# A gated feed-forward kernel: two sums moved up one place on VectorE, the last row tile copied out by two engines, and two late weight fetches split

## The chip, the cores and the metric

The kernel runs on one core of a Trainium2 chip. The metric is the device time of one execution, in microseconds (us). The 34 timed runs of the kernel before lie between 541.10 and 543.48 us, over all calls (a call is one session on one chip, in which kernels are timed in turn).

The engines are called PE (TensorE matmul), PEld (its weight loads, which overlap the matmuls), DVE (VectorE), ACT (ScalarE), POOL (GpSimd) and SP (SyncE, which issues all DMA transfers here). PSUM is the memory, in eight banks, into which PE writes its sums and out of which DVE and ACT read.

## The reference

```python
def reference(x, w_gate, w_up, w_down):          # x: 1 x 2048 x 1024, bf16; hidden size 3584
    g = jnp.einsum("bsd,df->bsf", x, w_gate)
    u = jnp.einsum("bsd,df->bsf", x, w_up)
    h = _gelu(g) * u                              # tanh form of gelu
    return jnp.einsum("bsf,fd->bsd", h, w_down)
```

## The kernel before

The kernel handles 1024 rows of `x` in each of two passes. It cuts every matrix product in 2 x 2 blocks and forms the four result blocks from seven block products in place of eight, with sums and differences of blocks made on DVE and POOL. A *unit* is such a 2 x 2 product for 256 hidden columns, for gate and up at once. A pass has 14 units and then the down-projection. In the code, `p1`, `u2` and `p5` are copies of PSUM banks that ACT makes (`snap`). "tb" and "sa" are operands of matmul products, and this document calls those groups of matmuls by them. A *keep cast* copies a block of `w_down` into a PSUM bank on ACT, and DVE then forms a difference from it (`keep_part`); there are three in a unit, in 12 units of the first pass. The parts that matter here (cuts are marked):

```python
    def unit(u, banks, xT, w, s, t, p1, after_p5, aside, keep, ahead_of_p4, snap_first):
        GU = range(2)                      # gate, up

        def add(ps, other):
            g = new(dve, ps[0], other[0], ADD, "sum", dtype=f32)
            dve(ps[1], ps[1], other[1], ADD)
            return g, ps[1]

        e, c, d = banks                    # three pairs of PSUM banks
        aside(-2)
        g, up = add(c, p1)                 # first block of this unit: the two sums
        ...
        for i in GU:
            product(e[i], s["s2"][i], t["t2"], False)
        ...
        keep(0, c[0])                      # first pass only
        ...                                # gelu(g), product g*up into hT
            u2 = [snap(e[i], "u2") for i in GU]
        keep(1, c[0])
        keep(2, c[1])
        c = d
        for i in GU:
            product(c[i], s["s1"][i], t["t1"], True)
        p5 = [snap(c[i], "p5") for i in GU]      # ACT copies the two banks out
        after_p5()
        for i in GU:
            product(e[i], s["s3"][i], t["t3"], False)
        ...
        for i in GU:
            product(c[i], s["s4"][i], t["tb"], False)   # adds onto the sums that p5 copied out
        times(2 * u + 1, 1, gelu(g), up)
        aside(1)
        g, up = add(c, u2)
        ahead_of_p4()                      # PE: first products of the next unit
        for i in GU:
            product(e[i], s["sa"][i], t["t4"], False)
        times(2 * u, 1, gelu(g), up)
        aside(2)
        times(2 * u + 1, 0, gelu(e[0]), e[1])    # the unit's last gelu and last product

    def keep_part(j, part, ps):            # differences of w_down blocks, made in the first pass only
        ...
        nc.scalar.copy(out=ps, in_=a)
        dve(made[j][:, part], ps, b, SUB)

    def fetch73(j):                        # one block of w_down, 256 KB, for each of j = 0 to 13
        raw[3, j] = slot([P, 2, N], bf16, "raw")
        nc.sync.dma_start(out=raw[3, j], in_=wdn[:, :, j, N:])

    # in down(), the last block of the output:
        def put21(i):
            store(ip, 1, i, 0, lambda st: nc.scalar.copy(out=st, in_=e[i]))

        if last:
            ...
            for i in I:
                for j in range(NJ):
                    matmul(e[i], sa[j][:, i * P : (i + 1) * P], q4[j], False, j == NJ - 1)
                put21(i)
```

DVE and PE run in the order in which the program is written. On ACT a scheduler sets the order, except in the very first unit.

## Time and profile before

| what | value | read from |
|---|---|---|
| time, median of 3 | 542.64 us (541.96 to 542.75) | the runs |
| span of the profiled run | 539.8 us | page |
| PE busy | 535.1 us, 99% | page |
| one unit, first pass | mostly 12.63 us | timeline, starts of the "sa" matmuls |
| one unit, second pass | 12.56 us | the same |
| last ACT copy, start and length | 536.37 us, 0.59 us | timeline |

The page's first part gives busy time, share of the span and number of instructions for each engine; its fourth part gives the chain of waits that ended last.

```profile
PE 535.1 (99%) x2414; PEld 379.5 (70%) x2414; DVE 334.9 (62%) x524; ACT 255.4 (47%) x463; POOL 239.2 (44%) x215
...
PE 99%; ACT 0%; DVE 0%; issue 0%
```

After the start PE is almost never visibly idle. That does not say that it is never late: the starts of its matmuls do. A unit is bounded by the first "sa" matmul of one unit and that of the next. The next view has the busy time of every engine in one unit of the first pass and in one of the second (columns: window, its length, then busy time and instructions of each engine, granted clock, DMA share, GB/s).

```profile
47.52:60.15 12.63, 12.63 (x59) 8.91 (x57) 8.36 (x14) 8.00 (x15) 12.63 (x12) 1.00 0.65 184
299.23:311.79 12.56, 12.56 (x58) 9.00 (x57) 6.56 (x11) 6.64 (x12) 9.05 (x9) 1.00 0.32 83
```

The same matmuls take 0.07 us longer in the first pass, where ACT and DVE have the keep casts and their differences to do as well. The timeline of that unit shows where (columns: start, length, engine, line, operation, output and input, count, and in brackets the idle time just before and what ended it).

```profile
48.83 0.60 ACT L179 ACTIVATE g<-bank 128x512 f32<-128x512 f32 x1 [1.48 <-PE bank L111]
...
49.82 0.69 DVE L90 TENSOR_TENSOR hT<-g,bank 128x512 bf16<-128x512 f32 x1 [1.75 <-PE bank L111]
...
50.42 0.68 DVE L90 TENSOR_TENSOR sum<-bank,p 128x512 f32<-128x512 f32 x1
...
51.14 0.59 ACT L274 CAST bank<-raw 128x512 f32<-128x512 bf16 x1 [1.71 <-DVE sum L90]
...
52.20 1.06 ACT L107 COPY u<-bank 128x512 f32<-128x512 f32 x2
...
53.14 1.12 ACT L274 CAST bank<-raw 128x512 f32<-128x512 bf16 x2
...
54.18 1.08 ACT L107 COPY p<-bank 128x512 f32<-128x512 f32 x2
54.89 1.70 PEld L111 LDWEIGHTS bank<-tb,s 128*128 128x128 f32 x8 [0.17 <-issue]
54.99 2.04 PE L111 MATMUL bank<-tb,s 128*128 128x512 f32 x8
```

Read it upwards. The weight load of the "tb" matmuls starts 0.17 us after the one before it ended, though the loads around it follow each other closely. The view names no releaser for this gap ("issue"), so what follows is read from the program. A load normally starts 0.22 us ahead of its matmul; here it is 0.10 (54.89 and 54.99), and about 0.07 us of the delay reaches the matmuls. The "tb" matmuls add into the banks that the p5 copies (54.18) read. Those stand on ACT behind two casts, two u2 copies, a gelu and the first cast (51.14), in one row without a gap. The first cast waited 1.71 us for DVE's sum, which ran at 50.42 because it stands behind the last product of the former unit (49.82), for which DVE had waited 1.75 us on PE.

The lines of the list of waits that belong to this (engine and line, what it waited for, us in total, times, longest):

```profile
DVE hT L90 <- PE bank L111: 43.7, 25, 1.8
...
ACT g L179 <- DVE sum L90: 28.6, 19, 1.7
...
ACT bank L274 <- DVE sum L90: 20.5, 12, 1.7
```

And the end of the kernel, from the timeline, and then SP's own wait for the last store (list of waits of SP's queue in the last 5 us):

```profile
536.37 0.59 ACT L413 CAST st<-bank 128x512 bf16<-128x512 f32 x1 [2.59 <-PE bank L111]
```

```profile
SPq L631 <- DMA out_dram<-st: 1.4, 1, 1.4
```

### The profile page before, as it was taken

To read this page: it belongs to the slowest core of one execution; us is meant where nothing else is said; L and a number is where in the kernel's file an instruction comes from. 1 tells how busy PE (TensorE), PEld (TensorE's weight loads), DVE (VectorE), ACT (ScalarE), POOL (GpSimd) and SP (SyncE) were. 2 spreads that over 40 slices of the span, in tenths; PEclk is the share of its full clock that TensorE was granted. 3 is DMA by queue.
4 is the path that set the end of the run, shared out by engine and by line. 5 is a ranking of instruction groups with operands and counts; after the bars stand their busy time and mean duration, and the time that the engine had idled before them with its cause. 6 is when DMAs were issued, how large, how long until landed. Compare 5 with 4: busy or idle time off the path is not lost.

```text
span 539.8 us, 7428 instructions
## 1 busy us (share of the span) xinstructions
PE 535.1 (99%) x2414; PEld 379.5 (70%) x2414; DVE 334.9 (62%) x524; ACT 255.4 (47%) x463; POOL 239.2 (44%) x215
## 2 busy tenths in 40 slices
PE   9999999999999999999999999999999999999997
PEld 5577777666677646888877667777777775488885
DVE  2986666666666895694945545445554459676730
ACT  3556666666656410255354555454555541114431
POOL 1079966677773500000097777777766600000000
PEclk9999999999999999999999999999999999999999
DMA  9766666666664899979772232233330059573751
GB/s 247 157 181 177 175 176 191 201 185 186 200 188 141 294 379 316 301 181 292 240 195 79 78 80 78 79 88 99 101 101 4 1 167 372 182 240 92 236 183 49
DMA packets 108133, 93.28 MB, mean 173 GB/s; under 512 B 17216, under 2 KB 92992, under 8 KB 108096
## 3 DMA queue, kind: packets, MB, share of 16 engines
q1 hardware_dynamic: 108096, 92.82, 58.8%
q8 instruction: 19, 0.31, 0.2%
q14 instruction: 18, 0.15, 0.1%
HBM read 74.45 MB, written 15.20 MB: 166 GB/s over the span
## 4 chain that ended last, share of the span: by engine, by line
PE 99%; ACT 0%; DVE 0%; issue 0%
PE bank L111 98%; PE bank L502 1%; PE bank L449 0%; ACT st L413 0%; DVE warm L433 0%
## 5 line engine op out<-in xcount | busy, mean ns | idle before, releaser
L93 POOL TENSOR_TENSOR s<-w 128x512 fp32r<-128x512 bf16 x102 | 120.0, 1198 | 165.1 <-DVE t L90 86.7
L111 PE MATMUL bank<-t,s 128*128 128x512 f32 x648 | 151.7, 390 | 0.0
L111 PEld LDWEIGHTS bank<-t,s 128*128 128x128 f32 x648 | 121.6, 188 | 25.5
L90 DVE TENSOR_TENSOR hT<-g,bank 128x512 bf16<-128x512 f32 x112 | 76.7, 687 | 92.9 <-ACT g L179 46.0
L111 PE MATMUL bank<-xT,w 128*128 128x512 bf16 (+1 forms) x504 | 111.9, 376 | 0.0
L107 ACT COPY p<-bank 128x512 f32<-128x512 f32 x124 | 70.6, 593 | 77.4 <-PE bank L111 77.1
L111 PEld LDWEIGHTS <-w 128*128 128x128 bf16 x504 | 47.0, 98 | 58.5 <-issue 6.9
L179 ACT ACTIVATE g<-sum 128x512 f32<-128x512 f32 x81 | 51.4, 635 | 29.8 <-DVE sum L90 28.6
L111 PE MATMUL bank<-q 128*128 128x512 f32 x240 | 58.9, 389 | 0.0
L111 PE MATMUL bank<-t,sa 128*128 128x512 f32 x216 | 58.8, 414 | 0.0
L93 POOL TENSOR_TENSOR s<-w,s 128x512 fp32r<-128x512 bf16 x50 | 57.8, 1181 | 0.0
L93 POOL TENSOR_TENSOR s<-s,w 128x512 fp32r<-128x512 f32 x50 | 57.0, 1162 | 0.0
L90 DVE TENSOR_TENSOR sum<-bank,p 128x512 f32<-128x512 f32 x54 | 37.0, 685 | 30.5 <-PE bank L111 30.5
L111 PE MATMUL bank<-tb,s 128*128 128x512 f32 x216 | 54.0, 392 | 0.0
L111 PEld LDWEIGHTS bank<-q 128*128 128x128 f32 x240 | 45.0, 188 | 9.4
L111 PE MATMUL bank<-raw,hT 128*128 128x512 bf16 x224 | 48.7, 379 | 0.0
L111 PEld LDWEIGHTS bank<-t,sa 128*128 128x128 f32 x216 | 40.7, 188 | 10.7
L111 PEld LDWEIGHTS bank<-tb,s 128*128 128x128 f32 x216 | 39.6, 188 | 9.9 <-issue 2.0
L102 ACT CAST tb<-raw 128x512 fp32r<-128x512 bf16 x28 | 17.2, 626 | 60.0 <-DMA raw<-in_w_down_dram 26.5
L90 DVE TENSOR_TENSOR q<-hT 128x512 fp32r<-128x512 bf16 x56 | 38.4, 686 | 4.5 <-PE bank L111 4.5
L111 PEld LDWEIGHTS <-hT 128*128 128x128 bf16 x224 | 21.8, 98 | 26.5 <-issue 0.5
L90 DVE TENSOR_TENSOR bank<-bank,p 128x512 f32<-128x512 f32 x54 | 37.4, 693 | 3.1 <-PE bank L111 3.1
(45 smaller groups left out, 454.7 us busy)
## 6 DMA issues: line engine op xcount, KB each, us to landing
raw<-in_w_down_dram SPq DMA_DIRECT2D x80, 256.0 KB, 4.8
q<-td SPq DMA_DIRECT2D x60, 256.0 KB, 5.0
w<-in_w_gate_dram SPq DMA_DIRECT2D x27, 512.0 KB, 5.9
w<-in_w_up_dram SPq DMA_DIRECT2D x27, 512.0 KB, 7.0
td<-m SPq DMA_DIRECT2D x12, 768.0 KB, 4.5
w<-td SPq DMA_DIRECT2D x6, 1024.0 KB, 9.7
out_dram<-st SPq DMA_DIRECT2D x32, 128.0 KB, 1.7
td<-w SPq DMA_DIRECT2D x2, 768.0 KB, 6.6
```

What stands on the lines that cost most here:

```text
L90: nc.vector.tensor_tensor(out=out, in0=a, in1=b, op=op)
L93: nc.gpsimd.tensor_tensor(out=out, in0=a, in1=b, op=op)
L102: nc.scalar.copy(out=t, in_=src)
L107: nc.scalar.copy(out=t, in_=ps)
L111: nc.tensor.matmul(ps, lhsT=lhs, rhs=rhs, start=start, stop=stop, skip_group_check=True)
L179: nc.scalar.activation(g, src, ACT.Gelu_apprx_tanh)
L502: nc.tensor.matmul(bank[3][:, :cols], lhsT=warm[:, :P], rhs=warm[:, :cols], start=True, stop=True)
```

## The change

Three small things, all meant to take waits off the path to PE or off the end. (1) The two sums that open a unit are recorded by the unit before it, ahead of its last product, so that DVE does them while it waits for PE. (2) The very last 128 x 512 copy out of PSUM is done half by ACT and half by DVE. (3) The last two of the fourteen `w_down` fetches of a stage are issued as two transfers each. The core of the diff:

```diff
-        g, up = add(c, p1)
+        g, up = c11()
 ...
         times(2 * u, 1, gelu(g), up)
-        aside(2)
+        behind_p4()
         times(2 * u + 1, 0, gelu(e[0]), e[1])
 ...
+            def behind_p4():
+                if "p1" in nxt:
+                    nxt["c11"] = add(cc, nxt["p1"])
+
+            def c11():
+                return nxt.pop("c11", None) or add(cc, p1)
 ...
     def fetch73(j):
         raw[3, j] = slot([P, 2, N], bf16, "raw")
-        nc.sync.dma_start(out=raw[3, j], in_=wdn[:, :, j, N:])
+        for kh in (range(2),) if j < NJ - 2 else (range(1), range(1, 2)):
+            kh = slice(kh.start, kh.stop)
+            nc.sync.dma_start(out=raw[3, j][:, kh], in_=wdn[:, kh, j, N:])
 ...
         def put21(i):
-            store(ip, 1, i, 0, lambda st: nc.scalar.copy(out=st, in_=e[i]))
+            def put(st):
+                h = N // 2 if last and i == NS - 1 else N
+                nc.scalar.copy(out=st[:, :h], in_=e[i][:, :h])
+                if h < N:
+                    nc.vector.tensor_copy(out=st[:, h:], in_=e[i][:, h:])
+
+            store(ip, 1, i, 0, put)
```

(`add` is moved out of `unit`, and `unit` takes `c11` and `behind_p4` as arguments; that is cut here.)

More of the change, by code (lines that the diff above doesn't have):

```diff
@@ L196, in raw_products, with add, unit @@
         return p1
-    def unit(u, banks, xT, w, s, t, p1, after_p5, aside, keep, ahead_of_p4, snap_first):
+    def add(ps, other):
+        g = new(dve, ps[0], other[0], ADD, "sum", dtype=f32)
+        dve(ps[1], ps[1], other[1], ADD)
+        return g, ps[1]
+    def unit(u, banks, xT, w, s, t, c11, after_p5, aside, keep, ahead_of_p4, behind_p4, snap_first):
         GU = range(2)
-        def add(ps, other):
-            g = new(dve, ps[0], other[0], ADD, "sum", dtype=f32)
-            dve(ps[1], ps[1], other[1], ADD)
-            return g, ps[1]
         e, c, d = banks
         aside(-2)
-        g, up = add(c, p1)
+        g, up = c11()
         aside(-1)
@@ L576 @@
             with tc.manual_schedule(engines={ENG.Activation}) if first else nullcontext():
-                unit(u, (e, cc, dd), xT, w, s, t, p1, prepare, aside, keep, ahead_of_p4, first)
+                unit(
+                    u, (e, cc, dd), xT, w, s, t, c11, prepare, aside, keep,
+                    ahead_of_p4, behind_p4, first,
+                )
             if u + 1 < NU:
```

## The prediction

> **What bounds the kernel.** TensorE: the page has PE busy 535.1 of 539.8 us, and the chain that ended last is 99% PE. The Trainium skill ("Perfetto Trace Analysis", Identifying the Most-Contended Engine) warns that pipelined matmuls make this busy time a poor measure, so I look at the starts of matmuls in the timeline. One f32 matmul of 512 columns starts every 0.227 us. Off that pace:
>
> - A unit takes 12.56 us in the second pass ("sa" matmuls at 299.23, 311.79 us) but mostly 12.63 in the first (47.52, 60.15, 72.78). The difference sits in the eight "tb" matmuls: 1.88 us in the first pass, 1.816 in the second; the "sa" group adds 0.01. In all about 0.75 us.
> - Only the first pass has the "keep" casts on ACT. From 51.14 us ACT has no gap: cast (after waiting 1.71 us for DVE's sum), gelu, two u2 copies, two casts, two p5 copies (54.18 to 55.26). The "tb" matmuls add into the banks that p5 empties; their weight load comes 0.17 us late ("issue") at 54.89. I infer that late p5 is the cause.
> - DVE's sum at 50.42 stands behind the last product of the former unit, for which DVE waited 1.75 us on PE, though the sum's own inputs were ready by about 47.
> - The end: the last ACT copy, 0.59 us at 536.37, then its store.
>
> **What the change does.** (1) The order of instructions has the two sums ahead of the last product on DVE in every unit; nothing is added. They should run at 48.0 to 49.3, in DVE's idle time; the last product can still run at 49.8. ACT's first cast moves to about 49.4 (behind the gelu at 48.83) and p5 to about 53.1, bounded then by PE's end of the u2 banks (about 51.5). That is 1 us of slack, so the "tb" stall vanishes: 0.7 us. In the second pass PE does not wait: nothing. (2) The last copy becomes 256 columns on ACT beside 256 on DVE. From 0.59 (ACT) and 0.69 us (DVE, two operands) for 512 columns and the clocks in "Trainium Kernel Development and Optimization", NeuronCore Architecture (1.2 and 0.96 GHz), halves are estimated at 0.38 and 0.42 us: 0.15 us off the tail. (3) The split fetches add four DMA issues, about 0.5 us each on SP; down-projection matmuls keep 0.907 us per four throughout, so no fetch is critical: zero.
>
> **On the critical path:** about 0.85 us, 0.16%. Predicted 541.8 us against 542.64; range 541.1 to 542.5. Faster by over 2%: 0.005; within 2%: 0.99; slower: 0.005.
>
> **What would show it.** First-pass units at 12.56 to 12.58 us, "tb" groups at 1.82; ACT's waits for DVE's sum (28.6 and 20.5 us in the list of waits) mostly gone; in that unit the first cast near 49.4 and p5 near 53.1; the last two copies near 0.4 us, ending within 0.1 us of each other; down-projection unchanged.
>
> **What would make it wrong.** The "tb" lag may not be p5's but come from shared memory ports or from DMA traffic; then only the tail gains. Two engines reading one PSUM bank at the end may slow each other, taking the 0.15 back. The spread of the runs (0.8 us) is as large as the effect: times alone may not show it, traces will.

## The result

The changed kernel took 541.64 us (median of 4, 541.34 to 541.75) against 542.67 for the kernel before in the same rounds (4 runs, 541.96 to 542.75). The ratio is 0.9983, with a 95% interval of 0.9966 to 1.0000. Ratios here and below are the mean time of one kernel's fast runs over that of the other's fast runs of the same rounds, so they are not quite the ratio of the medians. The mean difference is 0.92 us.

The profile after. First the page again:

```profile
PE 532.6 (99%) x2380; PEld 380.6 (71%) x2414; DVE 335.1 (62%) x525; ACT 259.9 (48%) x463; POOL 239.8 (44%) x215
...
PE 98%; DMA 1%; issue 0%; SPq 0%; DVE 0%; ACT 0%
```

PE seems to have 2.5 us less to do, but that is mostly a trap: 2380 matmuls are recorded in place of 2414, while the weight loads are still 2414. The edit takes no matmul away, so records are missing, not work. The second-pass units show it: they last 161.82 us in both traces, and PE's busy time in them falls from 161.82 to 161.00. About 0.78 of the 2.5 us is the wait that went away, which the profile had counted as busy, because it models the ends of matmuls (before, all 150.04 us of the first-pass units counted as busy). The durations of whole units do not suffer from missing records. The same two windows, one unit of each pass:

```profile
47.89:60.45 12.56, 12.49 (x58) 8.98 (x57) 8.39 (x14) 8.14 (x15) 12.56 (x12) 1.00 0.61 173
298.97:311.53 12.56, 12.49 (x57) 9.00 (x57) 6.47 (x11) 6.84 (x12) 9.03 (x9) 1.00 0.31 83
```

The first-pass unit now takes what the second-pass unit takes. The timeline of it (this kernel is 0.37 us later at this point, because its start was slower by about that much; subtract it to compare):

```profile
48.30 0.68 DVE L90 TENSOR_TENSOR sum<-bank,p 128x512 f32<-128x512 f32 x1
...
49.69 0.59 ACT L272 CAST bank<-raw 128x512 f32<-128x512 bf16 x1
...
50.18 0.69 DVE L90 TENSOR_TENSOR hT<-g,bank 128x512 bf16<-128x512 f32 x1 [0.59 <-PE bank L111]
...
53.45 1.08 ACT L107 COPY p<-bank 128x512 f32<-128x512 f32 x2
...
55.13 1.77 PEld L111 LDWEIGHTS bank<-tb,s 128*128 128x128 f32 x8
55.35 1.97 PE L111 MATMUL bank<-tb,s 128*128 128x512 f32 x8
```

The sum runs ahead of the product, DVE waits 0.59 us where it waited 1.75, the first cast no longer waits for a sum, p5 starts 1.1 us earlier in the unit (53.08 against 54.18 after subtraction), and the weight load of "tb" comes without a gap, 0.22 us ahead of its matmul. In the list of waits, in which the first cast's wait for the sum (20.5 us before) has gone:

```profile
DVE hT L90 <- PE bank L111: 13.6, 24, 0.6
...
ACT g L179 <- DVE sum L90: 7.6, 6, 1.7
```

The end, from the timeline, and then SP's own waits:

```profile
536.11 0.37 ACT L415 CAST st<-bank 128x256 bf16<-128x256 f32 x1 [2.59 <-PE bank L111]
536.51 0.42 DVE L417 CAST st<-bank 128x256 bf16<-128x256 f32 x1 [11.29 <-ACT st L415]
```

```profile
SPq L647 <- DMA out_dram<-st: 1.1, 1, 1.1
```

Two things are unlike the prediction. The halves of the last copy do not overlap: DVE was released by ACT (ACT's half raises semaphore 110, and DVE's half waits for it). And SP waits 1.1 us for the last store where it waited 1.4, although the store took as long to land as before.

Cut at the same events, the two spans compare like this. The stretches are: start to the first "sa" matmul; first-pass units, from there to the first down-projection matmul; first down-projection, from there to the first "sa" matmul of the second pass; second-pass units; second down-projection, to the start of the last copy; copy, from its start to the issue of the last store; end.

```
stretch (us)                 before   after   difference
start                         34.94   35.33    +0.39
first-pass units             150.04  149.26    -0.78
first down-projection        101.70  101.83    +0.13
second-pass units            161.82  161.82     0
second down-projection        87.87   87.88    +0.01
last copy to store's issue     0.61    0.86    +0.25
store's issue to end           2.80    2.53    -0.27
span                         539.78  539.50    -0.28
```

The start and the first down-projection vary from run to run in all kernels: 34.49 to 35.84 us and 101.70 to 102.46 us over fourteen traces. At the start PE waits for the first transfers. In the first down-projection it waits in some runs for late blocks of `w_down`, as in this line of the run `copy_only` below, which has another wait of this kind two microseconds later:

```profile
206.57 1.89 PE L111 MATMUL bank<-raw,hT 128*128 128x512 bf16 x7 [0.24 <-DMA raw<-in_w_down_dram]
```

This is the noise under which the change has to be seen. Left over from the change are three terms: -0.78, +0.25 and -0.27, in sum -0.80 us, beside the measured mean difference of -0.92.

### The profile page after: what moved, and what is told of

Read it like the earlier page. It is cut to its first block, busy times and chain, and to the rows that moved or that the text cites. A ratio compares the mean times of both kernels' runs of the same rounds, so it can differ in the third digit from the quotient of the medians.

```text
span 539.5 us, 7405 instructions
## 1 busy us (share of the span) xinstructions
PE 532.6 (99%) x2380; PEld 380.6 (71%) x2414; DVE 335.1 (62%) x525; ACT 259.9 (48%) x463; POOL 239.8 (44%) x215
## 4 chain that ended last, share of the span: by engine, by line
PE 98%; DMA 1%; issue 0%; SPq 0%; DVE 0%; ACT 0%
PE bank L111 98%; DMA xn<-in_x_dram 1%; PE bank L455 0%; SPq L448 0%; DVE st L417 0%; ACT st L415 0%; PE bank L508 0%
## 5 line engine op out<-in xcount | busy, mean ns | idle before, releaser
L90 DVE TENSOR_TENSOR hT<-g,bank 128x512 bf16<-128x512 f32 x112 | 75.5, 685 | 67.4 <-ACT g L179 50.7
L111 PE MATMUL bank<-xT,w 128*128 128x512 bf16 (+1 forms) x476 | 106.3, 375 | 1.9
L107 ACT COPY u<-bank 128x512 f32<-128x512 f32 x62 | 35.9, 590 | 23.7 <-PE bank L111 22.6
```

Source lines behind the costliest of these rows:

```text
L90: nc.vector.tensor_tensor(out=out, in0=a, in1=b, op=op)
L107: nc.scalar.copy(out=t, in_=ps)
L111: nc.tensor.matmul(ps, lhsT=lhs, rhs=rhs, start=start, stop=stop, skip_group_check=True)
```

## The experiments

Theory: the moved sums free the p5 copies (-0.78); the split copy costs time, because both halves read one PSUM bank (+0.25); and the split fetches save time only at the very end, through the turn that the last store gets among SP's closing waits (-0.27). Rivals are named with each run. All twelve runs, cut as above (each label is one kernel; the first two rows are the kernels above):

```
label           start  units1  down1  units2  down2   copy  end   span
before          34.94  150.04  101.70 161.82  87.87   0.61  2.80  539.78
after           35.33  149.26  101.83 161.82  87.88   0.86  2.53  539.50
sums_only       35.57  149.26  102.06 161.82  87.88   0.61  2.81  540.00
copy_only       35.39  150.04  102.46 161.82  87.87   0.86  2.79  541.23
fetch_only      35.06  150.04  101.70 161.82  87.88   0.61  2.53  539.64
sums_fetch      35.22  149.26  101.70 161.82  87.87   0.61  2.53  539.01
split_early     35.29  149.70  101.70 161.82  87.88   0.61  2.53  539.52
split_both      34.49  149.68  102.21 161.82  87.88   0.61  2.80  539.49
split_last      35.07  149.69  102.11 161.82  87.88   0.61  2.66  539.83
copy_two_banks  35.84  149.70  101.70 161.82  87.76   0.63  2.79  540.25
keeps_behind    35.41  149.49  101.71 161.82  87.87   0.61  2.80  539.71
before_late1    35.49  156.06  101.70 161.82  87.87   0.61  2.80  546.36
sums_late1      34.84  149.26  101.70 161.82  87.87   0.61  2.81  538.91
sums_late3      35.30  150.04  101.70 161.82  87.87   0.61  2.81  540.16
```

### Each part alone

`sums_only` is the diff above without its last two hunks, `copy_only` has the hunk of `put21` alone, `fetch_only` that of `fetch73` alone, and `sums_fetch` has all but `put21`. All four ran on one chip beside nine runs of the kernel before (median 542.15 us, 541.14 to 543.34).

> Of the three parts only the two sums are moved ahead of the last product. Theory (the p5 copies came late on ACT): the first-pass units from 35 to 185 us are 0.78 us shorter in total than before, every tb group back to 1.81 to 1.82 us, second pass unchanged, the end as before (last copy 0.59 us, four semaphore waits of SP after the one that sees the last store). Time 0.7 to 0.8 us less than before. Rival (all of the gain of the changed kernel comes from the tail or from run to run spread): units stay at 12.63 us, time as before.

Measured: 541.93 us, ratio 0.9989 (0.9975 to 1.0003). The first-pass units take 149.26 us, 0.78 less, all units at 12.56 us but the last; nothing else changed beyond the two noisy stretches. The time alone would not have shown it, as the interval includes 1; the stretch does.

> Only the last row tile's copy is split over ACT and DVE. Theory from the changed kernel's trace (both halves read one PSUM bank, so DVE is held until ACT has ended): ACT 0.37 us, then DVE 0.42 us, the last store is issued about 0.25 us later after the copy's start than before (0.86 against 0.61 us); time 0.2 to 0.3 us more than before. Rival, the prediction on record: the halves overlap, store issued 0.15 us earlier, time 0.15 us less.

Measured: 542.78 us, ratio 1.0007 (0.9994 to 1.0020). From the copy's start to the store's issue it takes 0.86 us and not 0.61. The rival, which is the prediction on record, has fallen.

```profile
537.59 0.37 ACT L415 CAST st<-bank 128x256 bf16<-128x256 f32 x1 [2.59 <-PE bank L111]
538.00 0.42 DVE L417 CAST st<-bank 128x256 bf16<-128x256 f32 x1 [11.29 <-ACT st L415]
```

> Only the two late weight fetches are split. Theory (the four additional transfers move the last store from the fourth to the eighth of the DMA semaphores that take turns, and SP at the end waits for these one after another): after the wait that sees the last store no further ones follow, where before there were four of about 0.062 us each; the end after the store's issue is 2.53 instead of 2.80 us, time 0.25 us less. Rival 1, the prediction on record: no effect. Rival 2 (the weights land earlier and something in the down projection moves up): down-projection stretches get shorter, the end stays at 2.80 us.

Measured: 542.15 us, ratio 0.9994 (0.9981 to 1.0007). The end takes 2.53 us and not 2.80, and no down-projection stretch is shorter than before. Both rivals have fallen.

> The changed kernel without the split copy. If the three parts add up: 0.78 from the units and 0.25 from the end, time 1.0 us less than before and 0.25 us less than the changed kernel; last store issued 0.61 us after its copy's start. If the split copy helped after all, slower than the changed kernel by 0.15 us.

Measured: 541.35 us, ratio 0.9981 (0.9969 to 0.9994), the one ratio below 1 whose interval is clear of it. All three stretches are where the parts put them: 149.26, 0.61, 2.53. By stretches this is 0.25 us better than the changed kernel, and 1.05 us better than before; it was not timed beside the changed kernel. So the best version here is the change without its split copy.

### What the split fetches do

In the built program the DMA transfers that SP issues take eight completion semaphores in turn. The last store has the fourth of them before and the eighth in the changed kernel, because four more transfers come ahead of it. The next three kernels change only which fetches are split:

```diff
-        nc.sync.dma_start(out=raw[3, j], in_=wdn[:, :, j, N:])
+        # split_early: j >= 2 in place of the condition below; split_both: 2 <= j < NJ - 2;
+        # split_last: j < NJ - 1
+        for kh in (range(2),) if j < NJ - 2 else (range(1), range(1, 2)):
+            kh = slice(kh.start, kh.stop)
+            nc.sync.dma_start(out=raw[3, j][:, kh], in_=wdn[:, kh, j, N:])
```

> The fetches of the first two weight blocks of that stage are split in place of the last two; the kernel is otherwise the one before. The number of transfers is that of the split late fetches. Theory (turn of the last store among the DMA semaphores): same gain as with the late ones, the end after the last store's issue 2.53 us, 0.25 us less than before. Rival (late weights arriving earlier): no gain, end 2.80 us.

> Both the first two and the last two fetches are split: eight additional transfers, so the last store is again the fourth of the eight semaphores. Theory: no gain, four more waits after the one that sees the store, end 2.80 us, time as before. Rival (late weights arriving earlier): gain of 0.25 us stays.

> Only the very last fetch of each pass is split: two additional transfers, so the last store takes the sixth of the eight semaphores. Theory (each semaphore that SP still has to check after the one that sees the store costs one wait of about 0.063 us): two further waits instead of four or none, the end after the store's issue 2.67 us, half way between 2.80 and 2.53; time 0.13 us less than before, which is under the noise. Rival (something else of the split fetches, on or off): 2.53 or 2.80.

Measured: the end takes 2.53 us with the early fetches split (last store on the eighth semaphore), 2.80 with both pairs split (on the fourth again) and 2.66 with one (on the sixth). Each is within 0.01 us of what the turn of the semaphore says, and it does not matter which fetch was split. The times (541.80, 542.03 and 542.07 us; ratios 0.9997, 1.0003 and 1.0011, all intervals about 1) can't resolve this. SP's records after the issue of the last store, as starts counted from it:

```
before      1.73  1.79  1.86  1.92  1.98 ... end 2.80     first of five waits sees the store
split_last  0.38  0.44  1.71  1.78  1.84 ... end 2.66     third
fetch_only  0.38  0.44  0.50  0.57  1.71 ... end 2.53     fifth
```

SP has five closing waits, one after another, each about 0.063 us. The store lands after 1.7 us in every case. If its semaphore is the last to be asked for, the four others have been passed by then; if it is the first, they still follow. In SP's own list of waits, first for `fetch_only` and then for `split_both`:

```profile
SPq L633 <- DMA out_dram<-st: 1.1, 1, 1.1
```

```profile
SPq L633 <- DMA out_dram<-st: 1.4, 1, 1.4
```

### What holds DVE in the last copy

The Trainium skill, "PSUM — Partial Sum Buffer", section "PSUM bank collisions raise a hardware error", says that the chip does not arbitrate when two engines access one bank in the same 32 partitions, two readers at disjoint columns included, but raises an error, so that software has to keep them apart; different banks are free. In the changed kernel DVE's half indeed waits for a semaphore of ACT's half, so it is the program that keeps the two apart; no run here had a collision. The next kernel keeps the shared output tile and gives each half its own bank:

```diff
                 for j in range(NJ):
+                    if i == NS - 1 and j == NJ - 1:
+                        matmul(c[0][:, : N // 2], sa[j][:, i * P : (i + 1) * P], q4[j][:, : N // 2], True, True)
                     matmul(e[i], sa[j][:, i * P : (i + 1) * P], q4[j], False, j == NJ - 1)
 ...
-            store(ip, 1, i, 0, lambda st: nc.scalar.copy(out=st, in_=e[i]))
+            def put(st):
+                h = N // 2 if last and i == NS - 1 else N
+                nc.scalar.copy(out=st[:, :h], in_=e[i][:, :h])
+                if h < N:
+                    nc.vector.tensor_copy(out=st[:, h:], in_=c[0][:, :h])
+
+            store(ip, 1, i, 0, put)
```

> Wrong result on purpose in the last 128 rows and 256 columns: one additional 256-column matmul goes into another PSUM bank just before the last one, and DVE's half of the copy reads that bank while ACT reads the first. Theory (one bank is what serialises the halves): DVE does not wait for ACT, the two overlap, each keeps its 0.37 and 0.42 us, the last store is issued about 0.4 us after ACT's start instead of 0.61 before and 0.86 with one bank; less the additional weight load of about 0.2 us, time within 0.1 us of before. Rival (the shared output tile or the engines' access to PSUM at large serialises them): DVE starts after ACT's end also here.

Measured: 541.58 us, ratio 0.9995 (0.9978 to 1.0012), and the result is wrong.

```profile
536.82 0.42 DVE L417 CAST st<-bank 128x256 bf16<-128x256 f32 x1 [10.78 <-PE bank L111]
537.06 0.37 ACT L415 CAST st<-bank 128x256 bf16<-128x256 f32 x1 [2.71 <-PE bank L111]
```

DVE is released by PE and not by ACT, and the two overlap for 0.18 us (537.06 to 537.24). The store is issued at 537.45, 0.39 us after ACT's start. So the halves have the lengths that the prediction gave them, and the wait goes with the shared bank (here also one PSUM tile), not with the output tile. A use for this is not at hand, as the last sums all lie in one bank. The skill's page also allows two engines in different quadrants (groups of 32 partitions) of one bank. Such a split would leave each copy at 512 columns; it was not tested.

### What delays the "tb" matmuls

`keeps_behind` leaves the sums where they were and takes two other instructions out of p5's way:

```diff
-        keep(1, c[0])
-        keep(2, c[1])
+        c0 = c
         c = d
         for i in GU:
             product(c[i], s["s1"][i], t["t1"], True)
         p5 = [snap(c[i], "p5") for i in GU]
+        keep(1, c0[0])
+        keep(2, c0[1])
         after_p5()
```

> The sums stay where they were; instead the second and third keep cast are put behind the p5 copies on ACT. Theory (late p5 copies stop the tb matmuls): p5 starts about 1 us earlier, at 53.2 where it was 54.2, tb groups back to 1.82 us, units 12.56 us, time 0.6 to 0.8 us less. Rival (the lag comes from memory ports or DMA traffic of the first pass, or from DVE's order itself): tb groups stay at 1.88 us.

Measured: 541.66 us, ratio 0.9998 (0.9981 to 1.0015). Eleven units of the first pass take 12.56 us each, without moving a sum. The p5 copies start at 53.59 us, and "tb" has no gap:

```profile
53.59 1.09 ACT L107 COPY p<-bank 128x512 f32<-128x512 f32 x2
54.54 1.14 ACT L275 CAST bank<-raw 128x512 f32<-128x512 bf16 x2
...
55.21 1.77 PEld L111 LDWEIGHTS bank<-tb,s 128*128 128x128 f32 x8
```

The casts, their traffic and DVE's order are all still there, and the lag is gone. So the rival of the expectation has fallen: late p5 copies cause the lag. The gain was smaller than expected for two reasons. The three unchanged first passes of the same call, `split_early`, `split_both` and `copy_two_banks`, take 149.68 to 149.70 us here and not 150.04, as does `split_last` on another chip (149.69): their units mostly take 12.59 to 12.62 us, so the lag is 0.03 to 0.06 us there in place of 0.07. What makes it differ between calls is open; the p5 copies start 6.66 us after the unit's first "sa" matmul in `before` and in `split_last` alike, so it is not the chain on ACT. And the last unit of the pass, which hands over to the down-projection, takes 9.37 us against 9.28 with the moved sums, and what follows it up to the first down-projection matmul another 0.14 us longer (1.96 against 1.82).

The other three kernels put additional ACT copies ahead of p5, in the first-pass units with keep casts:

```diff
+        for _ in range(1 if keeps() else 0):
+            nc.scalar.copy(out=warm, in_=u2[1])
         p5 = [snap(c[i], "p5") for i in GU]
```

`before_late1` has this in the kernel before, `sums_late1` in `sums_only`; `sums_late3` has one more ahead of `keep(1, ...)` and one ahead of `keep(2, ...)`.

> The kernel before, with one additional ACT copy of 0.57 us just before the p5 copies in every first-pass unit with keep casts. Theory (p5 is the last of a chain on ACT without slack): the additional work goes whole to TensorE, 0.5 to 0.6 us per unit, 12 units: 6 to 7 us more. Rival (lag from ports or traffic): under 1 us more.

Measured: 548.09 us, ratio 1.0113 (1.0095 to 1.0132): 6.2 us more. The first-pass units take 156.06 us, 6.02 more than 150.04 (12 x 0.50). The weight load of "tb" now comes late by 0.69 us:

```profile
55.82 1.08 ACT L107 COPY p<-bank 128x512 f32<-128x512 f32 x2
...
56.53 1.68 PEld L111 LDWEIGHTS bank<-tb,s 128*128 128x128 f32 x8 [0.69 <-issue]
```

> The same additional copy in the kernel with the moved sums. Theory: about 1.1 us of slack, so it is absorbed: time as with the moved sums alone, 0.7 us under before. Rival (ACT's load as such costs): 6 us more.

Measured: 541.15 us, ratio 0.9987 (0.9967 to 1.0006). The same copy costs nothing where the sums are moved: 149.26 us, to the hundredth what `sums_only` has. No matmul record is missing in this trace, and its "tb" groups take 1.82 us from their first matmul to the next group's (1.88 in most units before):

```profile
53.48 1.07 ACT L107 COPY p<-bank 128x512 f32<-128x512 f32 x2
...
54.64 1.77 PEld L111 LDWEIGHTS bank<-tb,s 128*128 128x128 f32 x8
```

Together these two say that p5 is the last link before PE in the kernel before, and that the moved sums gave it slack.

> Moved sums, three such copies before the p5 copies. They take 1.65 us, and the slack is estimated at 1.1 us (p5's first copy ends at 54.04, is needed by about 55.13): 0.5 to 0.6 us per unit too late, 12 units: 5 to 7 us more than before less 0.8, tb groups about 2.4 us. If the slack were larger, nothing; if it were gone, 18 us.

Measured: 542.29 us, ratio 1.0003 (0.9978 to 1.0028). The first-pass units take 150.04 us, only 0.78 more than `sums_only`: a miss by a factor of about seven. The trace says why:

```profile
54.47 0.59 ACT L107 COPY p<-bank 128x512 f32<-128x512 f32 x1
...
54.95 0.63 ACT L237 CAST warm<-u 128x512 bf16<-128x512 f32 x1
...
55.17 0.82 PEld L111 LDWEIGHTS bank<-tb,s 128*128 128x128 f32 x4
...
55.47 0.60 ACT L107 COPY p<-bank 128x512 f32<-128x512 f32 x1
...
56.18 0.76 PEld L111 LDWEIGHTS bank<-tb,s 128*128 128x128 f32 x4 [0.19 <-issue]
```

The scheduler put the third copy between the two p5 copies. So the first p5 copy came only 1.02 us later than in the changed kernel (54.47 against 53.45; the two units start within 0.03 us of each other), and the first four "tb" matmuls, into the first bank, came without a gap. The second p5 copy ended at 56.06, and the fifth weight load, for the second bank, was late by 0.19 us. The slack of the first copy is thus at least 1.02 us, in line with the estimate of 1.1. What was wrong was the delay that I thought I had put in.

## Why the prediction was right or wrong

The predicted 541.8 us and the range 541.1 to 542.5 hold the measured 541.64, and "within 2%" was right. But the sum of 0.85 us came out near the measured 0.80 partly by luck.

- **The sums (right).** Predicted: 0.7 us from the "tb" stall and 0.75 in all, units at 12.56 to 12.58 us, the first cast near 49.4, p5 near 53.1, nothing in the second pass. Measured: 0.78 us, 12.56 us, 49.32 and 53.08 (49.69 and 53.45 less the 0.37 us of later start), second pass 161.82 us in both. `sums_only`, `keeps_behind` and `before_late1` show that late p5 copies are the cause; on two later calls the lag to be won was only about 0.43 us (149.69 less 149.26), so the size of this gain is not the same everywhere.
- **"tb" groups at 1.82 us (right, but not read directly).** In the after trace the group's length to the next recorded matmul is 2.04 us in most units, because the first matmul behind it has no record. From the first to the eighth "tb" matmul it is 1.65 us in most first-pass units before and 1.59 after, as in the second pass; and `sums_late1`, which has the moved sums and all records, shows 1.82.
- **The last copy (wrong).** The step "halves are estimated at 0.38 and 0.42 us: 0.15 us off the tail" had the sizes right (0.37 and 0.42) and the sign wrong. The halves run one after the other: 0.86 us to the store's issue and not 0.61, 0.25 us lost. The prediction named slower readers of one bank as a risk; in fact they are not slower, the second is held. The skill's PSUM page has the rule, and I had not looked it up; and DVE's wait for ACT is written in the program.
- **The split fetches (wrong).** The step "no fetch is critical: zero" is right as far as it goes: no down-projection stretch moved. But it looked only at when weights arrive. A transfer also moves every later transfer on by one in the turn of eight semaphores, and so changes how many closing waits stand behind the last store. That gave 0.27 us, which the loss of the copy took back almost exactly.

The skill's warning that was quoted, "Perfetto Trace Analysis" on matmul busy time, proved its worth twice: PE's share was 99% in both kernels although 0.78 us of waiting went away, and its busy sum fell by 2.5 us mostly through missing records.

## What to carry to other kernels

An engine that is 99% busy can still be late by a few hundredths of a microsecond per step; compare the length of equal steps in two places, and where they differ, follow the instruction that was late upwards through the engines that feed it, until you find work that waited only because of its place in an order. Before you split an operation over two engines, ask whether both halves touch one PSUM bank, and read the waits that the program has between them. When a change moves the end by a few tenths, look at the closing waits too: the number of transfers ahead of the last store alone moved it by up to 0.27 us, so an unrelated edit may win or lose that much.

## What the Trainium skill lacked or had wrong

- "Runtime: NRT & Kernel Launch" lists stages after the kernel, but not the kernel's own closing waits on DMA semaphores, and none of the pages that I read has them. Here SP asks for five of them one after another at about 0.063 us each; with the last store on the fourth, sixth or eighth of eight semaphores the end takes 2.80, 2.66 or 2.53 us.
- "PSUM — Partial Sum Buffer", section "PSUM bank collisions raise a hardware error", has the rule. The runs show a program that keeps to it (DVE held until ACT's end with one bank, an overlap of 0.18 us with two); the error itself was not provoked. The section does not say what keeping the rule costs: two halves of 0.37 and 0.42 us take longer than one copy of 0.59 us.
- "Perfetto Trace Analysis", section "Optimizing Scalar/DVE Operations", gives about 51 ns of overhead for ScalarE on PSUM and about twice that, so about 0.10 us, in profiled latency. This ACT copy out of PSUM has more: from 0.59 us for 512 columns and 0.37 for 256 its fixed part is estimated at 0.15 us (2 x 0.37 less 0.59), so a half costs 63% of the whole.
- The section "Identifying the Most-Contended Engine" of the same page warns of pipelined matmuls, but not that records can be missing: 34 of 2414 in the after trace. In the second-pass units, which last 161.82 us in both traces, this lowered PE's busy time by 0.82 us. Why they are missing is not shown here.
